# The middle row of a Fourier layer: weighted by ScalarE, added by GpSimd and summed over partitions by six products, instead of made by 24 matmuls

## Chip, core and metric

The kernel runs on one NeuronCore of one Trainium2 chip. The core has five engines with a queue each, which run side by side and wait for one another by semaphores: TensorE (PE in the profile; its weight loads are PEld), VectorE (DVE), ScalarE (ACT), GpSimd (POOL) and SyncE (SP, which starts most DMAs). Each engine takes its instructions strictly in the order in which the program lists them. The metric is the device time of one execution in microseconds.

## What is computed

Two kinds of layers alternate on a sequence of S = 2048 rows of D = 640 numbers: attention (32 heads) and a Fourier layer. The part of the reference that matters here is the Fourier layer:

```python
a = einsum("bsd,ed->bse", x, dft_hid_re)
b = einsum("bsd,ed->bse", x, dft_hid_im)
y = einsum("ts,bse->bte", dft_seq_re, a) - einsum("ts,bse->bte", dft_seq_im, b)

x = x + attention(layernorm(x))
x = x + fourier(layernorm(x))
x = x + attention(layernorm(x))
x = x + fourier(layernorm(x))
```

All inputs and the result are float32.

## The kernel before

**Order.** The program is scheduled by hand: every engine runs its instructions in the order in which the Python code issues them. Two classes follow each attention: `Project` multiplies the attention's output by `wo`, adds the residual, takes the moments of each row and folds the rows; `Fourier` multiplies the folded rows by the DFT matrices.

**Folding.** The DFT matrices are symmetric, so rows s and S − s, and columns d and D − d, are first added and subtracted. `Project.run` goes over p = 0 to 7, a pair of row tiles each: `product` (TensorE, L1095 takes the result out by VectorE), `normal(k)` for an earlier pair k, `scale(k)` (ScalarE, L1136 to L1138, tile `na`), `moments(p)` (ScalarE squares at L1113, small GpSimd steps at L1110 to L1130, VectorE sums and differences at L1124 and L1125, tile `g`). `normal(k)` makes tile `fold` by two VectorE steps at L1150, and for k = 2, 3, 6 and 7 (q = 0 to 3) the sum and difference of two such tiles, `t[0]` and `t[1]` (L1155). These are split into a high and a low part: `split` copies the rounded value on ScalarE (L90) and subtracts it on VectorE (L91). The parts live in `xn0` to `xn7`, two for each q. The splits of q = 2 and q = 3 are the last work of `Project.run`.

**Products in three passes.** `three` (L96 to L98) multiplies such pairs: high by high, high by low, low by high.

**The Fourier loop.** `Fourier.run` goes over sixteen steps i, in the order m = 0, 1, 4, 5, 2, 6, 3, 7, 8, ..., 15 (`ORDER`). `accumulate(m)` adds nine products of block q = m mod 4 of the folded rows (stationary operand `xn`) with a piece of the DFT matrix (moving operand `chl`). `parts(i)` makes that piece from its raw load: a copy on ScalarE (L1291) and a subtraction on VectorE (L1293). In the loop's first four steps it is called six steps ahead: so the pieces of m = 3, 7, 8 and 9 are the first ScalarE instructions that follow the splits of q = 3. `turn` takes accumulated banks out of PSUM as `u`, and `hidden` multiplies `u` by the DFT matrix of the columns (`wh`).

**The middle row.** Rows S/4 and 3S/4, partition 0 of one tile, are mapped onto themselves by the folding and are handled apart. `edge` and `edge_sum` keep the input side of them in `e3` (high and low part in rows 0 and 1) and zero them in the tile. On the output side, `middle` makes the row in four steps, after m = 6, 7, 9 and 10: in steps 0 and 1, 18 and 6 matmuls (tile `pmid`) with one weight per partition as stationary operand (`mids`, 66 columns of which one matters) give one row, and VectorE adds `mm` times `e3` (L1331 to L1336) to make `um` in tile `c3raw`; in step 2, six products with a one (`pturn`, L1341) turn the row into columns, which are split into `uc` in `mids`; step 3 multiplies these by `wh`.

**Places.** `s.room` is tile `c3raw` of 1024 columns, first used by the edges. The place of `xn7` is used by `ea` in `edge` before the last split writes it. `xsq` is scratch of the squares of L1113. `midraw` holds the weights of the middle row, 128 partitions by 2 by 2 by 2, loaded during attention.

Of the kernel before, what the change touches and what calls it, by code (L numbers as in the profile page):

```python
# [5 lines left out]
F32 = mybir.dt.float32  # L6
F32R = mybir.dt.float32r
BF = mybir.dt.bfloat16
I32 = mybir.dt.int32
AF = mybir.ActivationFunctionType  # L10
OP = mybir.AluOpType
# [4 lines left out]
S, D, H, DH = 2048, 640, 32, 20  # L16
# [9 lines left out]
NQ = NT // 4  # L26
# [6 lines left out]
HD = D // 2  # L33
# [6 lines left out]
def mha_fnet_kernel(ctx, tc, x_in, wqk, wv, wo, seq, hid, nat_seq, nat_hid, out):  # L40
    nc = tc.nc
    V, A, G, PE = nc.vector, nc.scalar, nc.gpsimd, nc.tensor
# [31 lines left out]
    def bank(tag, shape, name):  # L74
        return pools["pool"].tile(list(shape), F32, name=name, tag=tag)
# [9 lines left out]
    def split(hl_h, hl_l, src, vector=False):  # L85

        if vector:
            V.tensor_copy(hl_h, src)  # L88
        else:
            A.activation(hl_h, src, AF.Copy)  # L90
        V.tensor_tensor(hl_l, src, hl_h.bitcast(F32), op=OP.subtract)  # L91

    def three(out_ap, pairs_h, pairs_l, start, stop):

        (ah, al), (bh, bl) = pairs_h, pairs_l
        PE.matmul(out_ap, ah, bh, start=start, stop=False)  # L96
        PE.matmul(out_ap, ah, bl, start=False, stop=False)  # L97
        PE.matmul(out_ap, al, bh, start=False, stop=stop)  # L98
# [15 lines left out]
    def moments(x, n, name, each=False):  # L114

        *_, rs = moment_steps(x, n, name, each)
        return rs
# [914 lines left out]
    class Project:  # L1032
# [111 lines left out]
        def normal(s, p):  # L1144
            if p not in s.na:
                s.scale(p)
            rs, g, nb, a = s.rs[p], s.g[p], s.nb[p], s.na[p]
            f = s.f[p] = s.room(f"f{p % 4}", [D], F32, "fold")
            for cols, r in ((slice(0, HD + 1), rs[:, 0, 1:2]), (slice(HD + 1, D), nb[:, 2:3])):
                V.scalar_tensor_tensor(f[:, cols], g[:, 1, cols], r, a[:, cols], op0=OP.mult, op1=OP.add)  # L1150
            if p - 2 not in FIRST:
                return
            q, t = FIRST.index(p - 2), (s.next.late("raw1", [D], F32, "fold2"), f)
            for k, op in enumerate((OP.add, OP.subtract)):
                V.tensor_tensor(t[k], s.f[p - 2], f, op=op)  # L1155
            for k in range(2):
                xn = s.next.keep(f"xn{2 * q + k}", [2, D], F32R, "xn")
                s.xn[q, k] = [xn[:, 0], xn[:, 1]]
                split(xn[:, 0], xn[:, 1], t[k])

        def run(s):
            s.ot[2] += s.heads(s.room, 2, (1,))
# [41 lines left out]
    class Fourier:  # L1204
# [50 lines left out]
        def edge_sum(s, step):  # L1255
            e, t, (h, l) = s.room[0:1, :D], s.ea, (s.e3[0:1, 0], s.e3[0:1, 1])
            if step == 0:
                V.tensor_tensor(e[:, :HD + 1], e[:, :HD + 1], t[:, :HD + 1], op=OP.add)
                V.tensor_tensor(e[:, HD + 1:], e[:, HD + 1:], t[:, HD + 1:], op=OP.subtract)
                A.activation(h, e, AF.Copy)  # L1260
                return
            V.tensor_tensor(l, e, h.bitcast(F32), op=OP.subtract)
            nc.sync.dma_start(s.e3[1:2, 0].bitcast(F32), h.bitcast(F32))
            nc.sync.dma_start(s.e3[2:3, 0].bitcast(F32), l.bitcast(F32))

        def mids(s):
            x = s.keep("mids", [4, 80], F32R, "mids")
            V.memset(x.bitcast(F32), 0.0)
            s.mid, s.uc = [x[:, 0], x[:, 1]], [x[:, 2], x[:, 3]]
            split(s.mid[0][:, :8], s.mid[1][:, :8], s.midraw.rearrange("p r k i -> p (r k i)"), vector=True)  # L1270


        ORDER = (0, 1, 4, 5, 2, 6, 3, 7) + tuple(range(8, 16))
# [42 lines left out]
        def middle(s, step):  # L1316

            if step == 0:
                s.um = s.room[0:1, :2 * HD + 2]
                s.pm = [bank(f"b{6 + ri}", [128, 512], "pmid")[:66] for ri in range(2)]  # L1320
            if step < 2:
                for ri, (k0, n) in enumerate(((0, HD + 2), (HD, HD))):
                    p = s.pm[ri][:, :n]
                    for q in (range(NQ - 1), (NQ - 1,))[step]:
                        j = NQ * ri + q
                        three(p, [s.mid[k][:, j:j + 66] for k in range(2)],
                              [x[:, k0:k0 + n] for x in s.pr.xn[q, ri]], q == 0, q == NQ - 1)
                    if step == 0:
                        continue
                    if ri == 0:  # L1330
                        V.scalar_tensor_tensor(s.um[:, :HD + 1], s.e3[0:1, 0, :HD + 1].bitcast(F32), s.mm[0:1, 0:1],  # L1331
                                               p[0:1, :HD + 1], op0=OP.mult, op1=OP.add)
                        V.scalar_tensor_tensor(s.um[:, :HD + 1], s.e3[0:1, 1, :HD + 1].bitcast(F32), s.mm[0:1, 0:1],
                                               s.um[:, :HD + 1], op0=OP.mult, op1=OP.add)
                    else:
                        V.tensor_copy(s.um[:, HD + 1:D], p[0:1, 1:])  # L1336
            elif step == 2:
                p = bank("b6", [128, 6], "pturn")
                for ri in range(2):
                    for c, (k0, n) in enumerate(FOLDS[ri]):  # L1340
                        PE.matmul(p[:n, 3 * ri + c:3 * ri + c + 1], s.um[:, k0:k0 + n], one[0:1], start=True, stop=True)  # L1341
                for ri in range(2):
                    for c, (_, n) in enumerate(FOLDS[ri]):
                        i = 3 * ri + c
                        split(s.uc[0][:n, i:i + 1], s.uc[1][:n, i:i + 1], p[:n, i:i + 1], i == 5)
            else:
                p = [bank(f"b{6 + ri}", [128, 512], "pmid")[:66, :HD + 2] for ri in range(2)]
                for ri in range(2):
                    for c, (_, n) in enumerate(FOLDS[ri]):
                        i = 3 * ri + c  # L1350
                        three(p[ri], [s.uc[k][:n, i:i + 66] for k in range(2)],
                              [s.w[ri, c][:n, k] for k in range(2)], c == 0, c == 2)
                s.ym = s.difference_and_sum(p, s.room[0:1, :3 * (HD + 2)], 1)
# [62 lines left out]
        def run(s, after):  # L1416

            s.x, s.acc, s.nb, s.next = {}, {}, 0, {}

            for tag, shape in [("wraw", [ND, 128])] + [(f"r{k}", [3 * (HD + 2)]) for k in range(2)] + [("x5", [2, D]), ("u2", [3, 512]),  # L1420
                                                                             ("u3", [3, 512])]:
                s.own(tag, shape, F32, "place")
            for i, m in enumerate(s.ORDER):
                tb, ri, q = m // 8, (m // 4) % 2, m % 4
                s.accumulate(m)
                if q == NQ - 1:
                    s.turn(tb, ri)
                if i < 4:
                    s.parts(i + s.AHEAD)
                elif i >= NQ + 2:  # L1430
                    s.parts(i + s.AHEAD - 2)
                if m in (6, 7, 9, 10):
                    s.middle((6, 7, 9, 10).index(m))
                if 11 <= m < 14:
                    s.hidden(m - 11)
                if m == 13:
                    s.hidden(3)
                    for t in (6, 7):
                        s.residual(t)
                if m in (12, 13) and s.dst is not out:  # L1440
                    k = m - 12
                    s.next[k] = moments([s.x[2 * k + i][:, 0] for i in range(2)], 2, "a")

                if 4 <= i < 10:
                    s.residual(i - 4)
                elif i == 10 and s.dst is not out:

                    s.wraw = [r(tag, [ND, 128], F32, "wraw") for r, tag in ((s.own, "wraw"), (s.late, "raw1"))]
                    for k in range(2):
                        nc.sync.dma_start(s.wraw[k], wqk[k * ND])  # L1450
            s.keep.close()
            begun = after(s)
            for k in range(2 if begun else 0):
                begun.q.early(k)
            for t in range(4, NP):
                s.hidden(t)
                if begun and t < 6:
                    begun.q.take(t - 4)
                elif begun:
                    begun.q.load(t - 4)  # L1460
# [159 lines left out]
    start = Pool("start", "right")  # L1620
# [8 lines left out]
    one = const.tile([128, 1], F32, name="one")  # L1629
    V.memset(one, 1.0)  # L1630
    zero = const.tile([128, 1], F32, name="zero")
# [80 lines left out]
```

## Time and profile before

| | |
|---|---|
| median of 3 runs | 2438.72 us (2437.7 to 2438.84) |
| span of the profiled execution | 2438.4 us |
| TensorE busy | 2417.5 us, 99% |
| ScalarE busy | 2115.4 us, 87% |
| VectorE busy | 1008.6 us, 41% |
| GpSimd busy | 546.6 us, 22% |
| first Fourier layer, from its first `pacc` product | 1154.48 us after the span's start |
| second Fourier layer, likewise | 2361.80 us |
| last VectorE step (L1410) | starts at 2429.20 us |

The profile is of one execution; of what lies around its span it shows nothing, and 2438.4 is 0.3 us under the median. Lines of the profile name an engine, a line of the kernel, an operation, and `out<-in` by the names of the tiles. A timeline row begins with the start and the duration in microseconds; several instructions alike and back to back are merged, with their count behind an x. In brackets stands how long the engine sat idle before, and whose end released it. Rows of groups give count, busy time in microseconds and the mean of one in nanoseconds. Matmuls overlap, so the time that one costs is read from start to start.

### The profile page before, as it was taken

To read this page: it belongs to the slowest core of one execution; us is meant where nothing else is said; L and a number is where in the kernel's file an instruction comes from. 1 tells how busy PE (TensorE), PEld (TensorE's weight loads), DVE (VectorE), ACT (ScalarE), POOL (GpSimd) and SP (SyncE) were. 2 spreads that over 40 slices of the span, in tenths; PEclk is the share of its full clock that TensorE was granted. 3 is DMA by queue.
4 is the path that set the end of the run, shared out by engine and by line. 5 is a ranking of instruction groups with operands and counts; after the bars stand their busy time and mean duration, and the time that the engine had idled before them with its cause. 6 is when DMAs were issued, how large, how long until landed. Compare 5 with 4: busy or idle time off the path is not lost. (4 is left out here: it accounts for less than half of the span.)

```text
span 2438.4 us, 43899 instructions
## 1 busy us (share of the span) xinstructions
PE 2417.5 (99%) x16264; PEld 1163.5 (48%) x16264; DVE 1008.6 (41%) x2272; ACT 2115.4 (87%) x2426; POOL 546.6 (22%) x1072
## 2 busy tenths in 40 slices
PE   9999999999999999999999999999999999999998
PEld 8544444543333332339884444454433333333596
DVE  7244442234343333427773444323333232333275
ACT  5699998899999999995457999988999999999862
POOL 3022221112212222115341212211211111222143
PEclk9999999999999999999999999999999999999999
DMA  6324231223222225318573332312221322252265
GB/s 211 121 88 127 84 111 54 77 68 113 72 94 90 88 89 161 102 39 295 187 233 104 108 101 93 110 54 70 82 81 57 92 63 69 57 154 78 76 242 198
DMA packets 130803, 267.88 MB, mean 110 GB/s; under 512 B 30976, under 2 KB 55328, under 8 KB 130580
## 3 DMA queue, kind: packets, MB, share of 16 engines
q1 hardware_dynamic: 90964, 162.51, 20.4%
q0 software_dynamic: 39616, 102.47, 13.3%
q8 instruction: 131, 2.15, 0.4%
q14 instruction: 92, 0.75, 0.1%
HBM read 174.63 MB, written 84.31 MB: 106 GB/s over the span
## 5 line engine op out<-in xcount | busy, mean ns | idle before, releaser
L613 ACT ACTIVATE e<-psc 128x1024 f32<-128x1024 f32 x2048 | 1917.3, 1060 | 108.0 <-PE psc L610 97.7
L621 PE MATMUL acc<-e,v 128*32 128x512 f32 x8192 | 1030.0, 600 | 0.4 <-DVE of L628 0.4
L610 PE MATMUL psc<-stq,stk 62*128 62x512 f32 x4096 | 743.1, 445 | 3.1 <-ACT e L613 2.2
L610 PEld LDWEIGHTS psc<-stq,stk 62*128 62x128 f32 x4096 | 334.5, 184 | 699.7 <-ACT e L613 546.0
L621 PEld LDWEIGHTS acc<-e,v 128*32 128x32 f32 x8192 | 210.2, 108 | 410.8 <-issue 378.1
L103 PE MATMUL pqk<-xt,wqk 128*128 128x512 f32 x1200 | 322.4, 410 | 1.2 <-DVE xt L91 0.7
L642 POOL DMA_DIRECT2D o<-oh x256 | 131.1, 521 | 826.0 <-DVE oh L637 814.3
L88 DVE CAST hl<-pqk 128x512 fp32r<-128x512 f32 x64 | 44.3, 692 | 599.4 <-PE pqk L103 599.4
L103 PEld LDWEIGHTS pqk<-xt,wqk 128*128 128x128 f32 x1200 | 215.1, 189 | 85.6 <-issue 38.0
L103 PE MATMUL pv<-wv,xt 128*128 128x320 f32 x960 | 151.7, 313 | 0.0
L103 PEld LDWEIGHTS pv<-wv,xt 128*128 128x128 f32 x960 | 141.0, 188 | 13.5 <-issue 10.2
L628 DVE STREAM_TRANSPOSE of<-acc 128x512 f32<-128x512 f32 x64 | 45.8, 715 | 225.7 <-PE acc L621 225.7
L642 POOL DMA_DIRECT2D o<-ot x256 | 128.2, 509 | 1.5 <-DVE c L88 0.6
L272 POOL DMA_DIRECT2D scrk<-hl x40 | 28.0, 700 | 398.0 <-DVE hl L91 253.6
L272 POOL DMA_DIRECT2D scrq<-hl x40 | 28.8, 720 | 367.9 <-DVE hl L91 237.6
L96 PE MATMUL py<-wo,o 128*128 128x320 f32 x320 | 101.0, 316 | 0.0
L891 DVE TENSOR_REDUCE far<-cq 128x1 f32<-128x512 f32 (+5 forms) x169 | 98.6, 584 | 5.7
L97 PE MATMUL py<-wo,o 128*128 128x320 f32 x320 | 98.7, 308 | 0.0
L98 PE MATMUL py<-wo,o 128*128 128x320 f32 x320 | 98.7, 308 | 0.0
L895 DVE TENSOR_TENSOR cq<-cq 128x512 f32<-128x512 f32 (+4 forms) x166 | 96.4, 581 | 3.8 <-DMA cq<-in_nat_seq_dram 3.2
L311 DVE COPY v<-pv 128x320 f32<-128x320 f32 x32 | 15.7, 490 | 161.2 <-PE pv L103 161.2
L281 DVE TENSOR_REDUCE top<-pn 32x1 f32<-32x512 f32 x50 | 33.7, 677 | 76.8 <-PE pn L280 76.6
(212 smaller groups left out, 1779.4 us busy)
## 6 DMA issues: line engine op xcount, KB each, us to landing
cq<-in_nat_seq_dram POOLq DMA_DIRECT2D x64, 512.0 KB, 5.2
scrq<-hl POOLq DMA_DIRECT2D x40, 512.0 KB, 3.8
scrk<-hl POOLq DMA_DIRECT2D x40, 512.0 KB, 3.2
stq<-scrq SPq DMA_DIRECT2D x256, 80.0 KB
stk<-scrk SPq DMA_DIRECT2D x128, 160.0 KB
o<-o SPq DMA_DIRECT2D x32, 384.0 KB
stq<-scrq SPq DMA_DIRECT2D x256, 40.0 KB
stk<-scrk SPq DMA_DIRECT2D x128, 80.0 KB
```

The lines of the kernel that those rows point to most:

```text
L96: PE.matmul(out_ap, ah, bh, start=start, stop=False)
L97: PE.matmul(out_ap, ah, bl, start=False, stop=False)
L98: PE.matmul(out_ap, al, bh, start=False, stop=stop)
L103: yield lambda i=i, j=j, k=k: PE.matmul(out_ap, a[i], b[j], start=dc == 0 and k == 0, stop=dc == ND - 1 and k == 2)
L272: G.dma_start(s.scr["qk"[k]][c * 128:(c + 1) * 128, :, tb * 512:(tb + 1) * 512], hl.bitcast(F32))
L610: PE.matmul(p[:, i], s.k[g, kc // 8, j][r, kc % 8 * 128:(kc % 8 + 1) * 128], s.q[g, qb, j][r], start=True, stop=True)
L613: A.activation(e, p, AF.Exp, scale=SCALE)
L621: PE.matmul(s.acc[32 * j:32 * j + 32], s.a.v[kc][:, v0:v0 + 32], s.e[n, j // 2][:, j % 2], start=kc == 0, stop=kc == NT - 1, skip_group_ch ...
L628: V.transpose(t0.rearrange("p b c -> p (b c)"), s.acc)
L642: G.dma_start(s.o[k, h * DH:(h + 1) * DH, qb * 512:(qb + 1) * 512], hl[k][32 * j:32 * j + DH])
L891: V.tensor_reduce(to, x, op=OP.max, axis=AX.X, apply_absolute_value=True)
L895: V.tensor_tensor(y, x, y, op=op)
```

## The change

A new method, `weigh(q, t)`, is called at the end of `normal` for each q. For both tiles `t[0]` (columns 0 to 320) and `t[1]` (columns 321 to 639) ScalarE multiplies each partition by its weight from `midraw`, into `um` for q = 0 and into `term` (or, for q = 3, into `c3raw`) after that; both lie in the place of `xn7`. For q = 1, 2 and 3 GpSimd adds the two 128x640 tiles: into `um` itself, into `xsq`, and into `c3raw`. `edge_sum(1)` adds `mm` times the edge to partition 0 of `um` on VectorE. `middle` keeps its last two steps, at their places after m = 9 and 10, and the six products `pturn` now sum over 128 partitions. `mids` holds `uc` alone.

```diff
@@ Project.normal
                 xn = s.next.keep(f"xn{2 * q + k}", [2, D], F32R, "xn")
                 s.xn[q, k] = [xn[:, 0], xn[:, 1]]
                 split(xn[:, 0], xn[:, 1], t[k])
+            s.next.weigh(q, t)
@@ Fourier.edge_sum
             V.tensor_tensor(l, e, h.bitcast(F32), op=OP.subtract)
+            m = s.um[0:1, :HD + 1]
+            V.scalar_tensor_tensor(m, e[:, :HD + 1], s.mm[0:1, 0:1], m, op0=OP.mult, op1=OP.add)
             nc.sync.dma_start(s.e3[1:2, 0].bitcast(F32), h.bitcast(F32))
             nc.sync.dma_start(s.e3[2:3, 0].bitcast(F32), l.bitcast(F32))
 
+        def weigh(s, q, t):
+
+            if q == 0:
+                x = s.keep("xn7", [2, D], F32, "um")
+                s.um, s.term = x[:, 0], x[:, 1]
+            to = s.room[:, :D] if q == NQ - 1 else s.term if q else s.um
+            for ri, cols in enumerate((slice(0, HD + 1), slice(HD + 1, D))):
+                A.activation(to[:, cols], t[ri][:, cols], AF.Identity, scale=s.midraw[:, ri, q // 2, q % 2:q % 2 + 1],
+                             bias=zero)
+            if q:
+                um = s.um if q == 1 else to if q == NQ - 1 else s.pr.room("xsq", [D], F32, "um")
+                G.tensor_tensor(um, s.um, to, op=OP.add)
+                s.um = um
+
         def mids(s):
-            x = s.keep("mids", [4, 80], F32R, "mids")
+            x = s.keep("mids", [2, 80], F32R, "mids")
             V.memset(x.bitcast(F32), 0.0)
-            s.mid, s.uc = [x[:, 0], x[:, 1]], [x[:, 2], x[:, 3]]
-            split(s.mid[0][:, :8], s.mid[1][:, :8], s.midraw.rearrange("p r k i -> p (r k i)"), vector=True)
+            s.uc = [x[:, 0], x[:, 1]]
@@ Fourier.middle
             if step == 0:
-                s.um = s.room[0:1, :2 * HD + 2]
-                s.pm = [bank(f"b{6 + ri}", [128, 512], "pmid")[:66] for ri in range(2)]
-            if step < 2:
-                for ri, (k0, n) in enumerate(((0, HD + 2), (HD, HD))):
-                    p = s.pm[ri][:, :n]
-                    for q in (range(NQ - 1), (NQ - 1,))[step]:
-                        j = NQ * ri + q
-                        three(p, [s.mid[k][:, j:j + 66] for k in range(2)],
-                              [x[:, k0:k0 + n] for x in s.pr.xn[q, ri]], q == 0, q == NQ - 1)
-                    if step == 0:
-                        continue
-                    if ri == 0:
-                        V.scalar_tensor_tensor(s.um[:, :HD + 1], s.e3[0:1, 0, :HD + 1].bitcast(F32), s.mm[0:1, 0:1],
-                                               p[0:1, :HD + 1], op0=OP.mult, op1=OP.add)
-                        V.scalar_tensor_tensor(s.um[:, :HD + 1], s.e3[0:1, 1, :HD + 1].bitcast(F32), s.mm[0:1, 0:1],
-                                               s.um[:, :HD + 1], op0=OP.mult, op1=OP.add)
-                    else:
-                        V.tensor_copy(s.um[:, HD + 1:D], p[0:1, 1:])
-            elif step == 2:
                 p = bank("b6", [128, 6], "pturn")
                 for ri in range(2):
                     for c, (k0, n) in enumerate(FOLDS[ri]):
-                        PE.matmul(p[:n, 3 * ri + c:3 * ri + c + 1], s.um[:, k0:k0 + n], one[0:1], start=True, stop=True)
+                        PE.matmul(p[:n, 3 * ri + c:3 * ri + c + 1], s.um[:, k0:k0 + n], one, start=True, stop=True)
@@ Fourier.run
-                if m in (6, 7, 9, 10):
-                    s.middle((6, 7, 9, 10).index(m))
+                if m in (9, 10):
+                    s.middle(m - 9)
```

## The prediction

> **What bounds the kernel now.** I read the page first, for the share of each engine, then the stretches of the two Fourier layers (busy time by windows), then the timeline of each engine there, and last the groups by shape for prices.
>
> ```profile
> span 2438.4 us, 43899 instructions
> PE 2417.5 (99%) x16264; PEld 1163.5 (48%) x16264; DVE 1008.6 (41%) x2272; ACT 2115.4 (87%) x2426; POOL 546.6 (22%) x1072
> ...
> 1167.00:1176.00 9.00, 9.00 (x47) 6.83 (x46) 6.09 (x10) 5.54 (x12) 0.00 (x0) 1.00 0.72 250
> ```
>
> The window row gives its length, then busy time of PE, PEld, DVE, ACT and POOL, the granted clock and the DMA. TensorE fills every microsecond of it, at full clock; GpSimd runs nothing from 1167 to 1176. So a matmul that goes is worth its full time as long as whatever follows it on TensorE is ready earlier. That is the whole question. The span, 2438.4, stands 0.3 under the median of the runs, 2438.72; I add differences to the median.
>
> **What goes.** The 24 products are 18 after row block m = 6 and 6 after m = 7.
>
> ```profile
> 1167.06 0.31 PE L96 MATMUL pmid<-xn,mids 128*66 128x322 f32 x1
> ...
> 1169.71 0.40 PE L96 MATMUL pacc<-chl,xn 128*128 128x512 f32 x1
> 1169.94 0.40 PE L97 MATMUL pacc<-chl,xn 128*128 128x512 f32 x1
> ...
> 1174.96 0.31 PE L96 MATMUL pmid<-xn,mids 128*66 128x322 f32 x1
> ...
> 1175.84 0.39 PE L96 MATMUL pacc<-chl,xn 128*128 128x512 f32 x1
> ...
> 2374.38 0.31 PE L96 MATMUL pmid<-xn,mids 128*66 128x322 f32 x1
> ```
>
> From start to start: 1169.71 − 1167.06 = 2.65 us and 1175.84 − 1174.96 = 0.88 us, so 3.53 per layer. The second layer repeats the same code on the same shapes 1207.32 us later (2374.38); I work in the first layer's times and double. Both layers: 7.06 us, 2431.7 if TensorE never waits. The three VectorE steps at L1331 to L1336 and the split in mids go too; the new scalar_tensor_tensor in edge_sum takes about their place. They lie beside TensorE's work in a stage where TensorE is the bound, so I cost these at nothing; only if VectorE ran late for the turned products would their going be worth something.
>
> **The six products** stay where they are; now 128 rows are summed instead of one.
>
> ```profile
> L610 PEld LDWEIGHTS psc<-stq,stk 62*128 62x128 f32 x4096 | 334.5, 184 | 699.7 <-ACT e L613 546.0
> L1341 PEld LDWEIGHTS pturn<-one,c3raw x24: 134/184/187, 1180.1 to 2388.5; 1*128 1x128 f32 x12, 1*65 1x65 f32 x8, 1*126 1x126 f32 x4
> ```
>
> A weight load of 128 columns takes 184 ns from one row and 184 from 62: rows are free. Between nothing and 0.1 us; I take nothing.
>
> **What comes: ScalarE.** Each layer gets eight activations, two per block q, of the kind of L1138 (Identity, a scale and a bias per partition, 320 columns).
>
> ```profile
> 1142.40 0.64 ACT L1138 ACTIVATE na<-g,zero,ars 128x319 f32<-128x319 f32 x1
> 1142.95 0.81 ACT L1113 ACTIVATE xsq<-xr,mean 128x640 f32<-128x640 f32 x1
> ```
>
> One occupies ScalarE 0.55 us and its result is there after 0.64. A pair: 1.10 us. Where do the four pairs fall?
>
> ```profile
> 1159.52 1.60 ACT L90 ACTIVATE xn<-fold 128x640 fp32r<-128x640 f32 x2 [1.41 <-DVE fold L1155]
> 1162.10 0.66 ACT L1136 ACTIVATE na<-g,nb,ars 128x321 f32<-128x321 f32 x1 [0.99 <-POOL nb L1129]
> ...
> 1165.28 1.60 ACT L90 ACTIVATE xn<-fold 128x640 fp32r<-128x640 f32 x2 [1.55 <-DVE fold L1155]
> 1166.79 2.18 ACT L1291 ACTIVATE chl<-craw 128x512 fp32r<-128x512 f32 x4
> ```
>
> Pair q = 2 follows the splits of 1159.52. Two splits occupy 1166.79 − 1165.28 = 1.51 us, so it runs from 1161.03 to 1162.13: it fills the idle 0.99 us exactly. Pair q = 3 has no cover. It stands between the splits and the four chl copies (1166.79), and the first chl is the very operand of m = 3. VectorE makes the other half of that chl (L1293); its folds (L1150) come ahead of the splits.
>
> ```profile
> 1157.61 0.55 DVE L1150 SCALAR_TENSOR_TENSOR fold<-g,ars,na 128x321 f32<-128x321 f32 x1
> 1158.07 0.55 DVE L1150 SCALAR_TENSOR_TENSOR fold<-g,nb,na 128x319 f32<-128x319 f32 x1
> ...
> 1162.03 0.20 POOL L1130 TENSOR_SCALAR nb<-ars 128x1 f32<-128x1 f32 x1
> ...
> 1163.29 0.56 DVE L1150 SCALAR_TENSOR_TENSOR fold<-g,ars,na 128x321 f32<-128x321 f32 x1 [1.30 <-ACT na L1137]
> 1163.83 0.55 DVE L1150 SCALAR_TENSOR_TENSOR fold<-g,nb,na 128x319 f32<-128x319 f32 x1
> ...
> 1167.65 2.49 DVE L1293 TENSOR_TENSOR chl<-craw,chl 128x512 fp32r<-128x512 f32 x4
> ...
> L1293 DVE TENSOR_TENSOR chl<-craw,chl 128x512 fp32r<-128x512 f32 x16 | 10.4, 680 | 0.2
> L1291 ACT ACTIVATE chl<-craw 128x512 fp32r<-128x512 f32 x32 | 18.5, 624 | 0.0
> ```
>
> Now chl is whole at about 1168.3, while the 18 products still keep TensorE until 1169.71: they were its cover. With ScalarE's pair alone: copy from 1167.89 to 1168.51, VectorE from 1168.56 to 1169.24. From the end of a VectorE step to the matmul that waits for it:
>
> ```profile
> 1183.47 0.15 DVE L91 TENSOR_TENSOR mids<-pturn,mids 65x1 fp32r<-65x1 f32 x1
> 1183.77 0.33 PE L96 MATMUL pmid<-wh,mids 128*66 128x322 f32 x1
> ```
>
> 0.15 us. So the second matmul of m = 3 would start at 1169.39 instead of 1169.94. Of the 2.65 us only 0.55 remain, and with the 0.88 a layer gains 1.43.
>
> **What comes: GpSimd.** Three adds of 128x640 per layer. No row has this shape; the nearest:
>
> ```profile
> L1407 POOL TENSOR_TENSOR xd<-xd,r 128x321 f32<-128x321 f32 x2 | 1.6, 804 | 0.1
> L1368 POOL TENSOR_TENSOR xd<-xd,r 128x321 f32<-128x321 f32 x16 | 14.2, 888 | 23.8 <-issue 13.9 <-DVE r L1360 8.9 <-PE phid L98 0.7
> L1369 POOL TENSOR_TENSOR xd<-xd,r 128x319 f32<-128x319 f32 x16 | 16.7, 1047 | 0.0
> L133 POOL TENSOR_TENSOR ars<-ars 128x2 f32<-128x2 f32 x12 | 2.3, 191 | 1.0
> ...
> 1188.60 0.74 POOL L1369 TENSOR_TENSOR xs<-xs,c3raw 1x319 f32<-1x319 f32 x1
> ```
>
> Twice 0.804 less one fixed part of 0.191 gives 1.42 us, which I take, since the L1407 pair ran while VectorE read PSUM. Ends: 2 x 0.74 − 0.19 = 1.29, and 0.888 + 1.047 = 1.94. Call it a.
>
> An add isn't hidden by running on an idle engine if it stops VectorE, and the trace shows that it does:
>
> ```profile
> 1192.74 0.48 DVE L1368 TENSOR_TENSOR xd<-xd,r 128x321 f32<-128x321 f32 x1
> 1192.96 0.86 POOL L1368 TENSOR_TENSOR xd<-xd,r 128x321 f32<-128x321 f32 x1 [3.63 <-DVE r L1360]
> 1193.14 1.04 DVE L1369 TENSOR_TENSOR xd<-xd,r 128x319 f32<-128x319 f32 x1
> 1193.79 1.12 POOL L1369 TENSOR_TENSOR xd<-xd,r 128x319 f32<-128x319 f32 x1
> ```
>
> VectorE's second add takes 1.04 instead of 0.48, and ends 0.36 after GpSimd's first has ended (1193.82); GpSimd's second ends 0.73 after that. They take turns, whole instructions at a time. The Trainium skill (SBUF — State Buffer, "Who interferes with whom") says that a VectorE instruction with two SBUF inputs and a GpSimd instruction that reads SBUF exclude each other; by it the sum is the one that follows, without it 1.43 a layer. The chl subtraction and the folds of L1150 both have two SBUF inputs.
>
> Add q = 2 starts when its pair has ended (1161.58 + 0.64, plus 0.05: 1162.28; GpSimd's own work is done by 1162.23) and lasts to 1162.28 + a. The fold due at 1163.29 waits for it, behind it the second fold, due at 1163.83, which now starts 0.46 after the add (the distance of the two unhindered folds, 1157.61 and 1158.07): D = 1162.28 + a + 0.46 − 1163.83 = a − 1.09 later, 0.33 us. The splits and chl on ScalarE wait for the folds and shift by D. (The split into xn7 also waits for this add, whose inputs lie in that tile; it is due two microseconds after the add's end.) Add q = 3 starts at 1166.79 + D + 0.55 + 0.64 + 0.05 = 1168.03 + D, half a microsecond before the chl copy ends, so GpSimd is first and VectorE waits: chl is whole at 1168.03 + D + a + 0.68, and the second matmul starts 0.15 later, at 1167.77 + 2a = 1170.61. That is 0.67 after today's 1169.94. Queued behind the add on GpSimd is only the copy of L1391, which isn't due before 1176; behind VectorE's wait stand three more chl, needed later.
>
> Per layer: +0.67 − 0.88 = **−0.21 us**; both, −0.42: 2438.3. Balance is at a = 1.53; at 1.29 it is −0.47 a layer (2437.8).
>
> **Pairs q = 0 and 1 and add q = 1** push the chain ScalarE, GpSimd, ScalarE of the moments later by about 2 us (pair 1.1, add and lock wait).
>
> ```profile
> 1156.23 0.83 ACT L1113 ACTIVATE xsq<-xr,mean 128x640 f32<-128x640 f32 x1 [1.83 <-POOL mean L1111]
> ```
>
> ScalarE has 1.83 us idle there, waiting for sums made from TensorE's last projection products, which do not move. I take 0; ends 0 and 0.5 a layer. No DMA is added, dropped or moved, so SP's queue is as it was. After this stage TensorE is again the bound to the end, so what a layer gains or loses goes through.
>
> **The rivals.** *VectorE isn't held at these places* (GpSimd comes later than I think, or chl goes first): −1.43 a layer, 2435.9. For it: places are half a microsecond apart; against: the four rows above. *Nothing is exposed*: 2431.7; needs chl 1.2 us earlier than now, for which nothing speaks. *The adds are slow* (slower than before): at a = 1.94 the second matmul starts at 1171.65, +1.71 − 0.88 = +0.83, and with 0.5 from the moments +1.33 a layer: 2441.4. It decides from a = 1.53. For it: the contended rows; against: L1407. *The clock falls*: TensorE idles from 1167.5 to 1170.6 but for one matmul.
>
> ```profile
> 0.00:20.00 20.00, 15.34 (x67) 12.56 (x68) 12.94 (x43) 11.99 (x19) 4.80 (x36) 0.91 0.77 274
> 2428.00:2431.00 3.00, 0.00 (x0) 0.00 (x0) 1.59 (x5) 0.00 (x0) 1.50 (x2) 0.90 0.75 287
> 2431.00:2434.00 3.00, 0.00 (x0) 0.00 (x0) 0.00 (x0) 0.00 (x0) 0.00 (x0) 0.50 0.51 179
> ```
>
> From 2428 TensorE is idle; 0.90 in three microseconds means 0.6 of them at 0.50, so the granted clock fell at about 2430.4, 2.4 us or more after the last matmul. At the start 0.09 of 20 us was missing, 1.8 us of full-speed work. If the two idle stretches counted as one of 3.1 us, each layer would lose 1.8: 2441.9. The one matmul between speaks against it. The Trainium skill (TensorE: Matmul & The Clock Gate, "What's actually happening") lets the clock fall after a whole idle window of about 3.4 us; by it nothing happens here.
>
> **How the numbers follow.** My forecast 0.57, VectorE not held 0.17, adds slow 0.14, clock 0.05, nothing exposed 0.04, others 0.03. A measurement of this kernel tells 0.2%, 4.9 us, from no change. Only "nothing exposed" lies beyond it on the fast side (0.04, 7.06 us); on the slow side slow adds and a fallen clock together (0.03). The range takes in the three likeliest: 2435.4 to 2441.9.
>
> **What would show it.** In the profile after: no pmid products from xn; TensorE idle before the second matmul of m = 3, that matmul 3.5 us after the place where the first pmid product stands today; the chl subtraction long, ending 0.6 to 0.7 us after GpSimd's add; the first L1150 of the last block long; adds of 1.3 to 1.6 us; m = 8 starting 0.2 us earlier than now relative to m = 6. If chl subtractions stay at 0.68, the lock is wrong and 2435.9 is due; if m = 3 follows m = 6 at once, all of it is wrong.

## The result, and the profile after

| | before | after |
|---|---|---|
| median | 2438.62 us, 5 runs | 2449.19 us, 5 runs (2446.10 to 2449.52) |
| ratio of after to before | | 1.0042, 95% interval 1.0030 to 1.0054 |
| span of the profiled execution | 2438.4 us | 2447.4 us |

The changed kernel is 10.6 us slower by the medians, 9.0 by the spans. The forecast was 2438.3, its range ended at 2441.9. It was wrong: of a loss beyond 4.9 us it had given 0.03 (slow adds and a fallen clock together).

The head of the page after: TensorE's busy time is as it was (2416.5 against 2417.5), though 48 matmuls are gone. Busy time hides the loss here: while the granted clock was 0.50, 12 matmuls filled five microseconds that 21 or 22 fill at full clock (below).

```profile
span 2447.4 us, 43825 instructions
...
PE 2416.5 (99%) x16216; PEld 1158.9 (47%) x16216; DVE 1011.4 (41%) x2264; ACT 2124.6 (87%) x2442; POOL 562.3 (23%) x1078
```

TensorE's waits after, over the whole span (what waited, for whom: us in total, times, longest). Neither of these two lines exists before:

```profile
PE pacc L96 <- ACT chl L1307: 8.2, 2, 4.1
...
PE pacc L97 <- DVE chl L1309: 2.0, 2, 1.1
```

TensorE's timeline after, first Fourier layer, from the end of m = 6:

```profile
1165.75 0.39 PE L98 MATMUL pacc<-chl,xn 128*65 128x512 f32 x1
1170.25 0.63 PE L96 MATMUL pacc<-chl,xn 128*128 128x512 f32 x1 [4.11 <-ACT chl L1307]
1171.97 0.79 PE L97 MATMUL pacc<-chl,xn 128*128 128x512 f32 x1 [1.09 <-DVE chl L1309]
1172.56 0.63 PE L98 MATMUL pacc<-chl,xn 128*128 128x512 f32 x1
1172.99 0.63 PE L96 MATMUL pacc<-chl,xn 128*128 128x512 f32 x1
...
1180.41 0.53 PE L97 MATMUL pacc<-chl,xn 128*65 128x512 f32 x1
1180.78 0.39 PE L98 MATMUL pacc<-chl,xn 128*65 128x512 f32 x1
```

Two losses stand here side by side. TensorE waits 4.11 + 1.09 us for the piece `chl` of m = 3, where the prediction had it wait about 3.1 in all. And the matmuls that follow are 0.43 us apart instead of 0.23, until 1180.78. The stretches of five microseconds after (length, then busy PE, PEld, DVE, ACT and POOL, granted clock, DMA) show why:

```profile
1165.00:1170.00 5.00, 1.14 (x5) 0.42 (x4) 4.28 (x6) 3.08 (x6) 0.41 (x2) 1.00 0.00 0
1170.00:1175.00 5.00, 3.66 (x8) 2.36 (x9) 3.49 (x4) 1.76 (x4) 1.37 (x1) 0.55 0.36 129
1175.00:1180.00 5.00, 5.00 (x12) 2.78 (x11) 2.86 (x5) 2.68 (x5) 0.00 (x0) 0.50 0.97 358
```

In the last row TensorE is busy throughout and runs 12 matmuls where, at 0.23 us apart, 21 or 22 fit: the granted clock is 0.50.

**The ledger.** All kernels run the same six steps of the loop (m = 0, 1, 4, 5, 2, 6) from the layer's first `pacc` product to the last of m = 6, in 12.3 us, so I count from that product, in each layer for itself. The numbers are starts, read from the timeline; "squares" is the first square (L1113) of the last round of `Project.run`, and `phid` the first product of `hidden`. "Low clock" is the time at granted clock 0.50 at this place, from stretches of one microsecond; one number where the layers agree.

| kernel | squares | second product of m = 3 | m = 8 | phid | low clock, layer 1 / 2 |
|---|---|---|---|---|---|
| before | 1.75 | 15.46 | 21.36 | 34.09 | 0 / 0 |
| after | 5.30 | 18.54 | 27.58 / 25.02 | 40.13 / 37.58 | 10.2 / 6.8 |
| e1, no adds | 1.75 | 14.78 | 22.96 / 19.93 | 35.45 / 32.49 | 6.8 / 0 |
| e2, last two blocks only | 1.75 | 15.84 | 24.01 / 20.96 | 36.52 / 33.52 | 6.8 / 0 |
| e3, pieces first | 5.30 | 16.67 | 23.12 / 25.58 | 35.65 / 38.11 | 3.4 / 10.2 |
| e4, 18 idle products | 5.30 | 18.54 | 26.73 / 25.06 | 39.24 / 37.62 | 6.8 / 3.4 |
| e5, add q = 1 on VectorE | 1.75 | 16.14 | 21.30 | 33.84 | 0 / 0 |
| e6, 39 idle products | 5.31 | 18.58 | 23.73 | 36.28 | 0 / 0 |
| e7, no GpSimd | 1.75 | 12.82 | 17.84 | 30.40 | 0 / 0 |
| e8, all adds on VectorE | 1.75 | 15.00 | 23.18 / 21.67 | 35.69 / 34.19 | 6.8 / 3.4 |
| e9, e5 with pieces first | 1.75 | 14.26 | 19.39 | 31.91 / 31.97 | 0 / 0 |
| e10, add behind the means | 1.74 | 16.12 | 22.83 / 21.25 | 35.36 / 33.78 | 3.4 / 0 |

After against before at phid: 40.13 − 34.09 = 6.04 and 37.58 − 34.09 = 3.49, together 9.53; the spans differ by 9.0. The wait accounts for 18.54 − 15.46 = 3.08 less 0.88 for the six products after m = 7, 2.20 a layer and 4.40 in all. The rest, 5.13, is the clock.

### The profile page after: what moved, and what is told of

The parts are those of the page before. It is cut to its first block, busy times and chain, and to the rows that moved or that the text cites. A ratio compares the mean times of both kernels' runs of the same rounds, so it can differ in the third digit from the quotient of the medians.

```text
span 2447.4 us, 43825 instructions
## 1 busy us (share of the span) xinstructions
PE 2416.5 (99%) x16216; PEld 1158.9 (47%) x16216; DVE 1011.4 (41%) x2264; ACT 2124.6 (87%) x2442; POOL 562.3 (23%) x1078
## 5 line engine op out<-in xcount | busy, mean ns | idle before, releaser
L103 PEld LDWEIGHTS pv<-wv,xt 128*128 128x128 f32 x960 | 141.0, 188 | 13.4 <-issue 10.2
```

What stands on the lines that cost most here:

```text
L103: yield lambda i=i, j=j, k=k: PE.matmul(out_ap, a[i], b[j], start=dc == 0 and k == 0, stop=dc == ND - 1 and k == 2)
```

## The experiments

Theory: the last blocks' moments are late because of what the change puts ahead of them, that makes `chl` of m = 3 late, and the clock falls on the wait. Rivals: the folds and pieces alone are late (VectorE, ScalarE), or the matmuls are slow because their operands are. "The last square" below is the column "squares". For e1 to e4 the median of before on the same chip was 2439.77, for e5 to e7 2438.20, for e8 and e9 2437.80, for e10 2438.83.

**e1: no adds.** Leaves out the three GpSimd adds, so the middle row holds block q = 3 alone.

```diff
-            if q:
-                um = s.um if q == 1 else to if q == NQ - 1 else s.pr.room("xsq", [D], F32, "um")
-                G.tensor_tensor(um, s.um, to, op=OP.add)
-                s.um = um
+            if q == NQ - 1:
+                s.um = to
```

> The changed kernel without GpSimd's three adds per layer; only the last pair of weighted columns goes on to the six products, so the middle row lacks the other three. The eight activations stay. Theory A (the adds do the harm: add q = 1 lengthens the moments' chain by some 3 us, adds q = 2 and 3 hold VectorE's fold and chl): TensorE's idle time after m = 6 falls from 4.1 us to under 2, the granted clock stays at 1.00 in both layers, and the time is that of the forecast without held VectorE, 2435 to 2437. Theory B (ScalarE's pairs do it, 1.1 us each on the chain): the idle time stays above 3.5 us, the clock falls, and the time stays above 2445.

Measured: 2438.78, ratio 0.9998 (0.9988 to 1.0007). The last square is back at 1.75: ScalarE's pairs alone delay the rounds before it by 1.1 and 1.9 us, and the 1.83 us of idle time that the prediction quoted take that up entirely. So without the adds the last moments aren't late, and theory A holds for them. The second product of m = 3 comes 0.68 earlier than before, but the clock, expected at 1.00, fell in the first layer all the same, after waits of 1.31 and 0.23 us, and the time missed the expected 2435 to 2437:

```profile
1166.27 0.49 PE L96 MATMUL pacc<-chl,xn 128*128 128x512 f32 x1 [1.31 <-ACT chl L1305]
1166.99 0.50 PE L97 MATMUL pacc<-chl,xn 128*128 128x512 f32 x1 [0.23 <-DVE chl L1307]
```

```profile
1165.00:1168.00 3.00, 1.50 (x5) 1.05 (x6) 2.22 (x4) 2.78 (x6) 0.00 (x0) 1.00 0.04 5
1168.00:1174.00 6.00, 6.00 (x14) 3.44 (x13) 3.44 (x7) 2.68 (x5) 0.00 (x0) 0.50 0.98 350
```

The second fence is e1's stretches: six microseconds at 0.50, with TensorE busy throughout.

**e2: only the blocks q = 2 and 3.** Leaves out pairs q = 0 and 1, the add q = 1 and the edge's share.

```diff
-            m = s.um[0:1, :HD + 1]
-            V.scalar_tensor_tensor(m, e[:, :HD + 1], s.mm[0:1, 0:1], m, op0=OP.mult, op1=OP.add)
...
-            if q == 0:
+            if q < 2:
+                return
+            if q == 2:
                 x = s.keep("xn7", [2, D], F32, "um")
-                s.um, s.term = x[:, 0], x[:, 1]
+                s.um = s.term = x[:, 1]
```

> The changed kernel without the pairs for q = 0 and 1, without add q = 1 and without the edge's step on VectorE; add q = 2 adds one tile to itself. So the middle row lacks two blocks and the edge. Theory A (the moments' chain is lengthened in rounds p = 4 and 5 and nothing else of the forecast is off by much): L1113 of the last round starts when TensorE's last projection products allow, as before the change; the second product of m = 3 comes 0.7 to 1.2 us later than before the change, relative to m = 6; the clock stays at 1.00; 2438 to 2440. Theory C (the pairs and adds at the tail are enough by themselves): idle above 3.5 us, fallen clock, 2445 or more.

Measured: 2441.53, ratio 1.0010 (1.0000 to 1.0020). The moments are as before (1.75) with two GpSimd adds left: those two don't lengthen the chain. With them and their pairs alone m = 3 comes 15.84 − 15.46 = 0.38 later than before, less than the 0.7 to 1.2 expected; the add q = 2, whose two inputs are one tile here, takes 1.25 us, where it takes 1.57 in the changed kernel. The clock fell in the first layer, which theory A had not expected.

**e3: the pieces first.** The first four loop steps and their `chl` pieces are issued ahead of `weigh(3)`.

```diff
+            if q == NQ - 1:
+                s.next.start()
             s.next.weigh(q, t)
...
+        def start(s):
+            s.acc = {}
+            for i in range(4):
+                s.accumulate(s.ORDER[i])
+                s.parts(i + s.AHEAD)
...
```

> The changed kernel with the first four loop steps and their pieces chl issued ahead of the pair and add of q = 3: TensorE's order is the same, ScalarE copies the four pieces first and weighs then, and GpSimd's last add cannot hold the first chl subtraction. Theory A (the lengthened chain of q = 0, 1 is about 2.7 us, the tail about 2.2): the chain is as late as in the changed kernel, the second product of m = 3 comes 1.6 to 2.0 us earlier than there; TensorE's idle time before m = 3 is about 3 us, at the edge of what lets the clock fall; 2439 to 2440 if it holds, 2443 to 2446 if it falls. Theory C (the tail is all): no idle time, 2432 to 2434.

Measured: 2445.62, ratio 1.0021 (1.0011 to 1.0031). The second product of m = 3 gains 18.54 − 16.67 = 1.87, what pair and add q = 3 cost. The moments stay late (5.30), TensorE still waits 3.04 us in one stretch, and the clock falls in both layers.

**e4: 18 more products after m = 6**, with results that nobody uses.

```diff
+                if m == 6:
+                    b = bank("b7", [128, 512], "fill")[:66, :HD]
+                    for _ in range(6):
+                        three(b, [x[:, :66] for x in s.uc], [x[:, :HD] for x in s.pr.xn[0, 0]], True, True)
```

> The changed kernel with 18 products put back after m = 6 whose result nobody reads (the old shapes, 66 and 320 columns). Nothing else is changed, so m = 3 waits for chl as in the changed kernel. Theory A (the idle time costs twice, once itself and once by the clock that it lowers for 5 to 10 us): the granted clock stays at 1.00, m = 3 starts at the same distance from m = 6 as in the changed kernel, and though 2.65 us of work are added per layer the time FALLS by 4 to 7 us, to 2442 to 2445. Theory D (the slow matmuls are not from idling but come with the wait itself or with other work at that time): matmuls of m = 3 and 7 still 0.43 us apart, time unchanged within 1 us, 2448 to 2450.

Measured: 2446.89, ratio 1.0031 (1.0019 to 1.0044). It decides nothing: the products cover only 2.6 us, waits of 1.47 and 1.22 remained, and the clock fell in both layers, so neither theory was put to the test. e6 does it in full.

**e5: the add q = 1 on VectorE.**

```diff
-                G.tensor_tensor(um, s.um, to, op=OP.add)
+                (V if q == 1 else G).tensor_tensor(um, s.um, to, op=OP.add)
```

> The add of block q = 1 runs on VectorE instead of GpSimd; everything else is the changed kernel. Theory A (the moments' chain of the last blocks is lengthened because GpSimd's 2.1 us add stands in GpSimd's queue and holds VectorE off): the last xsq of the layer returns to about 1.8 us after the first pacc product of the layer (changed kernel 5.3, before 1.75), the second product of m = 3 comes at about 15.8 (18.5 in the changed kernel), and the time falls to about 2438 to 2442. Rival B (any add at this place lengthens it, whichever engine does it, or ScalarE's pairs do): xsq stays at 4 or later, m = 3 at 17.5 or later, and the time is 2446 or more.

Measured: 2443.27, ratio 1.0019 (1.0010 to 1.0028). The squares come back to 1.75 and m = 3 to 16.14: one add of three on GpSimd accounts for 18.54 − 16.14 = 2.40 us a layer. What is left is the wait that the prediction worked out, 16.14 − 15.46 = +0.68 (forecast +0.67), and m = 8 and phid are 0.06 and 0.25 earlier than before (forecast 0.21). The time missed the expected 2438 to 2442. In the profiled execution the clock held through both waits:

```profile
1166.43 0.50 PE L96 MATMUL pacc<-chl,xn 128*128 128x512 f32 x1 [1.69 <-ACT chl L1307]
1168.15 0.50 PE L97 MATMUL pacc<-chl,xn 128*128 128x512 f32 x1 [1.22 <-DVE chl L1309]
```

```profile
1164.00:1169.00 5.00, 2.10 (x9) 1.07 (x8) 4.13 (x5) 3.91 (x7) 1.55 (x1) 1.00 0.00 0
1169.00:1174.00 5.00, 5.00 (x21) 3.19 (x20) 3.54 (x7) 3.26 (x7) 0.00 (x0) 1.00 0.94 265
```

This execution took 2438.39 us at a mean granted clock of 0.999 and is the fastest of the eleven; the other ten ran at 0.997 or 0.996 and took 2440.98 to 2444.90. A mean clock lower by 0.002 or 0.003 of the span is 5 to 7 us of TensorE's time, of the order of what they are longer by (2.6 to 6.5 us). That it fell at m = 3 in those ten is likely, since the waits are there, but no trace of them shows the place.

**e6: 39 more products** (13 times three, where e4 has six times three), enough to fill the whole wait.

> The changed kernel with 39 more products after m = 6, whose results nobody uses, so that TensorE hardly waits there. Theory A (part of the loss is the fallen granted clock after the waits at m = 3): the clock stays at 1.00 in both layers, m = 8 starts about 23.6 us after the first pacc product in both (27.6 and 25.0 in the changed kernel), and the time is about 2443 to 2445, some 5 us less than the changed kernel although TensorE does more work. Rival B (the matmuls after m = 3 are slow for another reason, such as their operands coming late): m = 8 stays at 25 or later and the time at 2448 or more.

Measured: 2443.86, ratio 1.0023 (1.0014 to 1.0032). m = 3 comes at the same moment as in the changed kernel (18.58, 18.54), but after it the clock is full, in e6's stretches:

```profile
1166.00:1171.00 5.00, 5.00 (x33) 4.34 (x32) 4.47 (x6) 3.07 (x6) 0.41 (x1) 1.00 0.00 0
1171.00:1176.00 5.00, 5.00 (x26) 3.44 (x24) 3.51 (x4) 2.19 (x5) 1.57 (x1) 1.00 0.35 116
1176.00:1181.00 5.00, 5.00 (x22) 3.65 (x22) 4.07 (x7) 4.18 (x9) 0.00 (x0) 1.00 0.87 310
```

Useless work makes the kernel 2449.19 − 2443.86 = 5.3 us faster; against the before of each it is +5.66 instead of +10.57, 4.9. m = 8 comes at 23.73 against 27.58 and 25.02, 3.85 and 1.29: 5.14, the 5.13 of the ledger. The rival (late operands) falls: the operands of m = 3 come as late as in the changed kernel, and the matmuls behind it run at full clock.

**e10: the add q = 1 on GpSimd, but two small steps later**, behind the two mean steps of that round.

```diff
             G.tensor_scalar(mean, mean, -1.0 / D, None, op0=OP.mult)
+            if getattr(s.next, "pending", None):
+                G.tensor_tensor(*s.next.pending, op=OP.add)
+                s.next.pending = None
...
+                if q == 1:
+                    s.pending = (um, s.um, to)
+                else:
+                    G.tensor_tensor(um, s.um, to, op=OP.add)
```

> The changed kernel with the GpSimd add of q = 1 issued two small instructions later: behind the two mean steps (L1110 and L1111 of the changed kernel) of that round, where GpSimd waits some 2.9 us for ScalarE's squares anyway. Same engine, same add. Theory A (the add lengthens the moments' chain because it stands ahead of the means in GpSimd's queue): xsq of the rounds after it comes back to about -10.4, -3.8 and 1.75 us relative to the first pacc (-8.7, -1.3 and 5.3 in the changed kernel), the second product of m = 3 at about 16.1 (18.5), and the time is about 2443, as with that add on VectorE. Rival B (GpSimd and VectorE holding each other off is what lengthens the chain, wherever the add stands): the last xsq stays at 3.5 or later, m = 3 at 17.5 or later, and the time is 2446 or more.

Measured: 2441.25, ratio 1.0015 (1.0005 to 1.0025). The squares are at 1.74 and m = 3 at 16.12, as with the add on VectorE. The time is 2.4 us above before (e5: 5.1, with the same waits within 0.02 us); the nine executions lie far apart, 2438.68 to 2448.67. GpSimd around the add in the changed kernel, with the VectorE subtraction beside it and the square on ScalarE that waits:

```profile
1141.60 2.14 POOL L1280 TENSOR_TENSOR um<-um 128x640 f32<-128x640 f32 x1
...
1142.23 2.06 DVE L1309 TENSOR_TENSOR chl<-craw,chl 128x512 fp32r<-128x512 f32 x1
...
1143.71 0.63 POOL L1110 TENSOR_TENSOR mean<-rowsum 128x2 f32<-128x2 f32 x1
...
1144.42 0.23 POOL L1111 TENSOR_SCALAR mean<-mean 128x2 f32<-128x2 f32 x1
...
1144.69 0.83 ACT L1113 ACTIVATE xsq<-xr,mean 128x640 f32<-128x640 f32 x1 [1.60 <-POOL mean L1111]
```

The means, whose inputs VectorE had finished by 1136.6, stand behind the add, and the squares wait for the means: ScalarE idles 1.60 us. The add and the subtraction hold each other up besides: each takes over 2 us, where the add takes 1.57 and the subtraction 0.68 elsewhere. And in e10 (its L1113 is the add, its L1116 the square):

```profile
1140.05 0.68 POOL L1111 TENSOR_SCALAR mean<-mean 128x2 f32<-128x2 f32 x1
1140.70 1.99 POOL L1113 TENSOR_TENSOR um<-um 128x640 f32<-128x640 f32 x1
1143.30 0.19 POOL L1118 TENSOR_SCALAR sumsq<-sumsq 128x2 f32<-128x2 f32 x1 [0.61 <-ACT xsq L1116]
```

```profile
1141.36 0.81 ACT L1116 ACTIVATE xsq<-xr,mean 128x640 f32<-128x640 f32 x1
...
1142.30 0.83 ACT L1116 ACTIVATE xsq<-xr,mean 128x640 f32<-128x640 f32 x1
```

The add takes 1.99 us, hardly less than the 2.14, but now lies beside the two squares, where GpSimd would wait for ScalarE anyway, and still has 0.61 us left when it is done. It is the add's place in GpSimd's queue that cost 2.4 us a layer (18.54 − 16.12), not the add's length.

**e8: all three adds on VectorE** (`V.tensor_tensor` for `G.tensor_tensor` in `weigh`).

> The changed kernel with all three adds on VectorE (one letter), nothing else. Theory A (the adds cost by running on GpSimd: its queue and its turns with VectorE): the last xsq stays at 1.75 us after the first pacc product, no fold or chl subtraction is held, the second product of m = 3 comes at about 15.2 (15.46 before, 16.1 with only the add q = 1 on VectorE), phid about 1.2 us a layer earlier than before, so about 2.4 below before where the granted clock holds; the waits of some 1.3 and 0.9 us stay, so the clock may still fall in some executions and the median lie between 2436 and 2440. Rival B (VectorE has no room, three adds of 0.83 us delay folds and pieces): m = 3 at 16.5 or later and the time at 2443 or more.

Measured: 2439.21, ratio 1.0003 (0.9994 to 1.0012). m = 3 at 15.00, 0.46 earlier than before: VectorE has room, and having the adds q = 2 and 3 on GpSimd, longer and in turns with VectorE, had cost 16.14 − 15.00 = 1.14. But waits of 1.32 and 0.45 us are left, and the clock fell in both layers; phid is 1.6 and 0.1 us later than before, although the waits alone would make it 1.3 earlier.

**e9: e3 and e5 together.** Pieces first, add q = 1 on VectorE, the other two on GpSimd.

> The four loop steps and their chl pieces ahead of weigh(3), as in the run with the pieces first, and the add q = 1 on VectorE; the adds q = 2 and 3 stay on GpSimd. Theory A (the delay of m = 3 is two sums: the lengthened moments' chain, and pair and add q = 3 ahead of chl): both go, the second product of m = 3 comes at about 14.3 us after the first pacc (16.7 with the pieces first alone, 16.1 with the add q = 1 on VectorE alone), TensorE waits under 1.8 us in all, phid is about 2 us a layer earlier than before, and the time about 4 below before where the clock holds. Rival B (the two parts are one and the same delay): m = 3 at 15.8 or later, and the time at or above before.

Measured: 2435.09, ratio 0.9987 (0.9978 to 0.9996). m = 3 at 14.26 as expected: the two delays add up. TensorE still waits 0.57 and 0.45 us, and in this profile the clock held there; the two layers' phid come 4.3 us earlier together. By the medians the gain is 2.7; the interval, 1.0 to 5.4 us, includes both.

**e7: no GpSimd, pieces first and the first ones earlier.** Pair q = 0 on ScalarE, q = 1 by two VectorE steps that multiply and add in place, q = 2 on ScalarE, q = 3 on ScalarE behind the pieces; two VectorE adds after the loop's fourth step; the first two loop steps and their pieces are issued between the last two blocks. The squares' scratch and `um` move to other places too, so e7 shows what the change can be worth, not which of its edits brings it.

```diff
...
+            f = s.next
+            f.acc = {}
+            for i in range(2):
+                f.start(i)
+                f.parts(i + f.AHEAD, (0,))
+            s.normal(NP - 2)
+            for i in range(2):
+                f.parts(i + f.AHEAD, (1,))
+            s.normal(NP - 1)
...
+                if q == 1:
+                    V.scalar_tensor_tensor(s.um[:, cols], t[ri][:, cols], w[:, ri], s.um[:, cols], op0=OP.mult, op1=OP.add)
+                else:
+                    A.activation(to[:, cols], t[ri][:, cols], AF.Identity, scale=w[:, ri], bias=zero)
+
+        def gather(s):
+            V.tensor_tensor(s.um, s.um, s.term, op=OP.add)
+            V.tensor_tensor(s.room[:, :D], s.room[:, :D], s.um, op=OP.add)
...
```

> The middle row without GpSimd: pair q = 0 on ScalarE, q = 1 by two VectorE scalar_tensor_tensor that add in place, q = 2 on ScalarE into a place of its own, q = 3 on ScalarE after the four loop steps and their chl pieces, and two VectorE adds at the end; the first two loop steps and their pieces are made ahead of the last two blocks. Theory A (the loss comes from the waits of VectorE and GpSimd for each other and from the pair q = 3 ahead of chl, and from the clock that falls on the wait): TensorE doesn't wait at m = 3, the clock stays at 1.00, m = 8 starts 3.5 us earlier than before relative to the first pacc (about 17.8 instead of 21.4) and the time is about 7 us below before, 2431 to 2434. Rival B (VectorE's or ScalarE's added work lengthens the moments' chain all the same): xsq of the last block is later than 2.5, m = 3 comes at 14 or later, and the time is 2436 or more.

Measured: 2432.36, ratio 0.9973 (0.9963 to 0.9982). TensorE's timeline in e7 between m = 6 and m = 3 (128*65 is the last of m = 6, 128*128 the first of m = 3):

```profile
1165.39 0.39 PE L98 MATMUL pacc<-chl,xn 128*65 128x512 f32 x1
1165.62 0.39 PE L96 MATMUL pacc<-chl,xn 128*128 128x512 f32 x1
1165.86 0.39 PE L97 MATMUL pacc<-chl,xn 128*128 128x512 f32 x1
```

No wait at all, no fallen clock there, and m = 8 at 17.84 against 21.36: 3.52 a layer, the 24 products' whole price. At phid it is 3.69 a layer, 7.4 in all; the medians say 5.8, the interval 4.4 to 9.0. It is the fastest version here, 5.8 us under its before, where the changed kernel stood 10.6 above.

## Why the prediction was wrong

**Right: what goes.** 3.53 us a layer was forecast for the 24 products; e7, where nothing waits, shows 3.52. The six products' weight loads take 190 ns (the median) with 128 rows, 184 with one: nothing, as forecast.

**Right, with luck in the sum: the pair q = 3 has no cover, and VectorE and GpSimd take turns.** The rows of the changed kernel:

```profile
1163.66 1.57 POOL L1280 TENSOR_TENSOR um<-um 128x640 f32<-128x640 f32 x1
1164.76 0.83 DVE L1150 SCALAR_TENSOR_TENSOR fold<-g,ars,na 128x321 f32<-128x321 f32 x1 [1.92 <-ACT na L1137]
...
1169.82 1.55 POOL L1280 TENSOR_TENSOR c3raw<-um,c3raw 128x640 f32<-128x640 f32 x1 [4.59 <-ACT c3raw L1276]
1170.23 3.49 DVE L1309 TENSOR_TENSOR chl<-craw,chl 128x512 fp32r<-128x512 f32 x4 [0.78 <-ACT chl L1307]
```

The first fold takes 0.83 instead of 0.56, and the four subtractions 3.49 instead of 2.49, the extra microsecond being the first one's wait for the add. The rule of the Trainium skill that the prediction weighed (SBUF — State Buffer, "Who interferes with whom") agrees with this. The adds took 1.57 and 1.55 by their rows where 1.42 was taken, the folds came 0.30 later in e5 (0.33 forecast), and the sum at m = 3, +0.67, is +0.68 in e5. That it agrees to 0.01 is luck. In e5 the add q = 3 starts 0.11 later than forecast and takes 0.13 longer, but the subtraction ends 0.55 after it, not 0.68, and the matmul starts 0.05 after that, not 0.15. By the prediction's own formula adds of 1.55 us would have made the kernel slower than before.

**Wrong: "Pairs q = 0 and 1 and add q = 1 ... I take 0; ends 0 and 0.5 a layer."** This is the step that failed. The pairs do cost nothing (e1), but the add costs 2.40 us a layer (e5, e10). The prediction looked at one idle time, ScalarE's 1.83 us in the last round, against a delay of some 2 us put down once. But the add stands ahead of the two means in GpSimd's queue, and the squares wait for the means. Against before, the squares of the last three rounds come 1.1, 1.9 and 0 us later with the pairs alone (e1), and 2.8, 4.3 and 3.6 us later in the changed kernel (first layer). The prediction named the in-order queue for the add q = 3 and said what stands behind it; for the add q = 1 it didn't ask.

Why the idle 1.83 us take up only 0.7 of the 4.3, where they took up all of 1.9 in e1, can be read from the last round. Its squares follow `na` of the round before in ScalarE's queue, and `na` waits for GpSimd's `nb`. First the changed kernel, then e1:

```profile
1154.12 0.53 POOL L1115 TENSOR_SCALAR sumsq<-sumsq 128x2 f32<-128x2 f32 x1 [2.87 <-ACT xsq L1113]
...
1155.83 0.82 DVE L1125 TENSOR_TENSOR g<-xr 128x638 f32<-128x638 f32 x1
...
1155.91 0.79 POOL L1123 COPY g<-xr 128x4 f32<-128x4 f32 x1
...
1157.20 0.66 ACT L1136 ACTIVATE na<-g,nb,ars 128x321 f32<-128x321 f32 x1 [3.17 <-POOL nb L1129]
```

```profile
1150.52 0.19 POOL L1115 TENSOR_SCALAR sumsq<-sumsq 128x2 f32<-128x2 f32 x1 [1.99 <-ACT xsq L1113]
...
1151.73 0.19 POOL L1123 COPY g<-xr 128x4 f32<-128x4 f32 x1
...
1152.42 0.66 ACT L1136 ACTIVATE na<-g,nb,ars 128x321 f32<-128x321 f32 x1 [1.98 <-POOL nb L1129]
```

In e1 the pairs have used up the idle time: the last squares start at 1153.96, right behind `na`, and their means are ready at 1153.93. So whatever delays the chain further is paid in full. In the changed kernel the squares of the round before come another 2.4 us later, and from the start of L1115 to that of `na` it takes 3.08 us instead of 1.90, for GpSimd's steps now fall beside VectorE's folds and sums: the 0.79 us of L1123 end 0.05 us after the VectorE difference beside it. 2.39 + 1.18 = 3.57, and the last squares are 3.55 late.

**Wrong: the clock rival's condition.** Given 0.05, because "the one matmul between speaks against it" and two stretches would have to count as one of 3.1 us. e1 shows the fall with 1.54 us of idle time, and e8 with 1.77: the two stretches do add up where they lie in one cell of a grid of 3.4 us (last section). The price, 1.8 us a layer, was also too small: the changed kernel loses 5.13 in the two. The range ended 3.3 us above before. With the moments in time and the clock falling in part of the executions, the median is 5.1 us above before in e5 and 2.4 in e10; with the moments late and the clock held (e6) it is 5.7. So either error can put the time outside the range by itself, and the late moments do.

**Its marks.** m = 8 was to start 0.2 us earlier; it starts 6.2 and 3.7 later. The long chl subtraction and the long fold are there, and the second product of m = 3 stands late, as it said: the signs were of the right mechanism at the wrong size. The range took in the three likeliest cases, and in none of them did the moments cost more than 0.5 us a layer.

## What to carry to other kernels

A long instruction on an engine that runs chains of tiny steps is priced by what stands behind it in the queue, not by that engine's idle share: look for the place where the engine waits for another one anyway, and put it there (e10: one add moved behind two small steps, 2.4 us a layer). Work taken off the bounding engine is only worth something if nothing waits in its place, and on TensorE a wait can cost twice, once as idle time and again in the half clock that may follow; two gaps of 1.31 and 0.23 us were enough for that (e1). When an execution's profile looks better than the median of its runs, read the granted clock of the others before believing it.

## What the runs showed of the hardware

**The clock falls after short gaps, by steps of 3.4 us, and how they lie in a grid of that step matters.** Waits at m = 3 in the two steps (first layer), and the low clock that followed in the two layers: 0.57 + 0.45 us (e9), none; 1.31 + 0.23 (e1), 6.8 and 0; 1.32 + 0.45 (e8), 6.8 and 3.4; 1.38 + 1.22 (e2), 6.8 and 0; 1.67 + 1.23 (e10), 3.4 and 0; 1.69 + 1.22 (e5), none in the profile; 1.47 + 1.22 (e4), 6.8 and 3.4; 3.04 + 0.44 (e3), 3.4 and 10.2; 4.11 + 1.09 (after), 10.2 and 6.8. All the low stretches at this place are one, two or three times 3.4 us. Within one execution they begin on one grid: in e3 at 13.55, 85.23, 1170.67, 2378.99 and 2437.01 us, which lie 21, 318, 354 and 17 times 3.413 us apart. So it matters how a wait lies in the grid. In e10 the waits of the two layers are alike, but in the first both lie in one cell of the grid, TensorE is idle for 2.90 us of it and the clock falls at its end; in the second they are parted over two cells, 1.55 and 1.34 us, and it holds (e10's cells, columns as above):

```profile
1164.53:1167.94 3.41, 0.51 (x3) 0.20 (x2) 2.58 (x3) 3.18 (x7) 1.55 (x1) 1.00 0.00 0
1167.94:1171.35 3.41, 3.41 (x8) 2.16 (x8) 1.74 (x3) 0.00 (x0) 0.00 (x0) 0.50 0.66 235
2372.85:2376.26 3.41, 1.86 (x9) 1.00 (x7) 2.60 (x4) 3.02 (x6) 0.31 (x1) 1.00 0.00 0
2376.26:2379.67 3.41, 2.07 (x8) 1.41 (x9) 3.31 (x4) 1.63 (x4) 1.24 (x1) 1.00 0.13 31
2379.67:2383.08 3.41, 3.41 (x15) 2.02 (x14) 1.98 (x4) 1.56 (x3) 0.00 (x0) 1.00 1.01 333
```

Counted like this in all traces, at this place a full clock fell after every cell with 1.71 us of idle time or more, and held after every cell with 1.69 us (e5) or less but one, 1.55 us (e1). So about half a cell was enough here. Elsewhere less was: the fall of before at 85.45 us followed a cell with 1.1 us of idle time, so idle time alone isn't the whole rule. The Trainium skill (TensorE: Matmul & The Clock Gate, "What's actually happening") gives a free-running window of 3413 ns, with which this grid agrees; but the idle window that it requires before the clock falls did not occur at m = 3 in any of these runs. Why the clock stays low for two or three cells while TensorE is busy, no run here settles.

**The same kernel, unchanged, varies too, and its clock falls too.** Across the before runs of these comparisons the time goes from 2435.68 to 2441.51; before's own profile has 3.4 us at low clock at 13 to 18 us and again at 85 to 89, e5's has neither.

**A GpSimd add of 128x640 fp32** took 1.54 to 1.58 us at q = 2 and 3 (1.25 in e2, where both inputs are one tile), and 1.85 to 2.14 at q = 1; on VectorE in e5 it takes 0.83:

```profile
1139.66 0.83 DVE L1280 TENSOR_TENSOR um<-um 128x640 f32<-128x640 f32 x1 [0.25 <-ACT um L1276]
```
